# Hash attention and a gated feed-forward block: keys and queries of pairs one to four turned by VectorE from block loads, and another pace of weight pieces

## Chip, cores and metric

The kernel runs on one core of one Trainium2 chip. The metric is the device time of one execution in microseconds, as a median of several runs. Engines are named as the profile names them: PE is TensorE's matmul, PEld its weight load, DVE VectorE, ACT ScalarE, POOL GpSimd, SP SyncE; SPq and the like are the queues in which an engine issues its DMAs.

## What is computed

The inputs q, k and v have 4 batches, 8 heads, 768 positions and 64 columns. Each query and key gets a bucket from the signs of six projections, and attends only within its bucket. The result is rearranged to 3072 tokens of 512 columns and goes through a gated block with 1536 hidden columns.

```python
q_bits = (np.einsum('bhsd,dk->bhsk', q, proj) > 0)      # k_bits likewise
mask = q_bucket[:, :, :, None] == k_bucket[:, :, None, :]
scores = np.where(mask, scale * np.matmul(q, k.transpose(0, 1, 3, 2)), -1e9)
attn = softmax(scores)                                   # over the keys
x = np.matmul(attn, v).transpose(0, 2, 1, 3).reshape(B * S, H * D)
g = x @ w_gate
out = (g * (1.0 / (1.0 + np.exp(-g))) * (x @ w_val)) @ w_out
```

The three weights come as doubles. The kernel reads them as two 32-bit words per number and makes float parts of them itself.

## The kernel before

**Attention.** Two heads at a time make a pair; there are 16 pairs, numbered 0 to 15, four to a batch (`pairs`, L309). Each pair runs through these steps.

- `fetch` (L312) loads raw q, k and v. q and k have one buffer each (`bufs=1`, L323), v has two. For pairs 0 to 4 (`n <= NP`, L326) q and k come as rows, two DMAs a tensor, with runs of 64 floats. For pairs 5 to 15 (L332 to L340) they come in blocks of 32 by 32, four DMAs a tensor with runs of 32 floats, laid so that turning each block gives the operand with head and column on the partitions.
- `front(n)` (L420) returns the steps that make the operands. For pairs 0 to 4 `transpose` (L421) makes three 128x128 transposes on PE (L426) for each half of q and k, twelve a pair, and ACT copies each half out of PSUM (L429). For pairs 5 to 15 `transpose_blocks` (L478) turns q and k with one DVE instruction each (L480).
- `hash_next` (L468) projects q and k (four matmuls, L439) and ACT takes the signs (L444). The bits of q are copied to the second head's rows by a DMA in SP's queue (`spread_q`, L456). Those of k are written twice by ACT with a mask for pairs 1 to 4 (L475), and once by ACT and then spread by DVE (`spread_k`, L450 to L453) for pairs 5 to 15. Pair 0 has its own step, `hash_own` (L458).
- `score` (L502) multiplies q and k, adds the product of the bits in the same PSUM bank, and ACT takes the exponential (L515) into a ring of twelve units. There are twelve units a pair: two halves of the queries by six blocks of keys.
- `add` (L540) sums the exponentials on DVE (L547, L551, L554) and `total` (L559) sums them over the partitions on PE (L565). The sums go through SP's queue (`few`, L570), a reciprocal on DVE (L574), memory (`sums`, L576), and back, spread over the partitions (L583).
- `attend` (L518) multiplies the weights by v (av, L526). `norm` (L587, L590) scales the result, and for the first 1024 tokens `split` (L263) cuts it into three parts, with L283 on ACT and L287 and L292 on DVE.

**The order** is written out by hand and each engine works its queue in that order. The loop over pairs (L612) emits for pair n: the turn of pair n + 1 if that is DVE's, twelve scores with the adds between them, the turn if it is PE's, the total of pair n - 1, the hashing of pair n + 1, norm and reciprocal of earlier pairs, weight pieces, and av of pair n. The loads of pair n + 2 are emitted after the third score where DVE turns pair n + 1 (L628), and after PE's transposes otherwise (L632).

**Weight pieces.** There are 36 pieces. `load_words` (L119) reads one (L126), `scale` (L128) scales it on ACT (L135, L136), `widths` (L145) joins the words on DVE (L149, L151, L154), `round_up` (L139) rounds on ACT (L142), and `parts` (L159) makes the remaining parts on DVE (L162, L164) and writes the piece to memory (L166). So a piece has a first half of three DVE instructions, and in the next pair a second half of two. `PACE` (L609) says how many pieces are begun in each pair; 23 pieces are made in the attention. The other 13 are made in the gated block by `turns` (L212), a few steps after each atom of work. During attention POOL's queue issues the reads and writes of the pieces, and, in the last three pairs, reads of ring pieces (`bring`, L234, L244).

**Gated block** (L664). Three blocks of 1024 tokens. For each of the twelve groups of hidden columns the products `a` and `n` are made, and after every three groups the product `o`, all at L681.

Of the kernel before, what the change touches and what calls it, by code (L numbers as in the profile page):

```python
# [8 lines left out]
FP32 = mybir.dt.float32  # L9
# [10 lines left out]
def kernel(  # L20
# [20 lines left out]
    nc = tc.nc  # L41
    PSUM = bass.MemoryType.PSUM
    B, H, S, D = q.shape
    NBITS = proj.shape[1]
    P = 128
# [3 lines left out]
    BLOCK = 32  # L49
    NP = H // 2  # L50
# [12 lines left out]
    OFF = 2.0**35  # L63
# [234 lines left out]
    def attention(scope):  # L298
# [13 lines left out]
        def fetch(n, name, queue, half=None):  # L312
            b, pr = pairs[n]
            if name == "v":
                t = raws["v", n] = raw.tile([P, 2, NCH, D], FP32, tag="vraw", name="vraw")
                queue.dma_start(
                    t.rearrange("p h c d -> p h (c d)"),
                    v[b, 2 * pr : 2 * pr + 2].rearrange("h (p c) d -> p h (c d)", c=NCH),
                )
                return  # L320
            src = q if name == "q" else k
            if not half:
                raws[name, n] = raw.tile([P, NCH, 2, D], FP32, tag=name + "raw", name=name + "raw",  # L323
                                         bufs=1)
            t = raws[name, n]
            if n <= NP:  # L326
                cs = slice(None) if half is None else slice(half * CH, (half + 1) * CH)
                for h in range(2):
                    queue.dma_start(t[:, cs, h, :],
                                    src[b, 2 * pr + h].rearrange("(p c) d -> p c d", c=NCH)[:, cs, :])  # L330
                return
            blocks = t.rearrange("p c a b -> p (c a b)").rearrange(  # L332
                "p (c a d) -> p c a d", a=P // BLOCK, d=BLOCK)
            for h in range(2):
                for x in range(D // BLOCK):
                    at = h * D + x * BLOCK
                    queue.dma_start(  # L337
                        blocks[at : at + BLOCK],
                        src[b, 2 * pr + h][:, x * BLOCK : (x + 1) * BLOCK].rearrange(
                            "(a p c) d -> p c a d", c=NCH, p=BLOCK))  # L340

        def load(n, names):
            if n < len(pairs):
                for name in names:
                    fetch(n, name, nc.sync)
# [22 lines left out]

        HR = 16
        assert 2 * NBITS <= HR and 2 * HR == BLOCK  # L370
        rules = fixed.tile([BLOCK, 8, BLOCK], FP32, tag="rules", name="rules")
        NUDGE = -(2.0**-120)
        nc.gpsimd.memset(rules[:, 2:8, :], 0.0)
        nc.gpsimd.memset(rules[:, 0:2, :], NUDGE)
        groups = rules.rearrange("p x (g r) -> p x g r", r=HR)
        nc.gpsimd.memset(groups[:, 0, :, NBITS : 2 * NBITS], 1.0)
        nc.gpsimd.memset(groups[:, 1, :, NBITS : 2 * NBITS], -1.0)
        for h in range(2):
            nc.gpsimd.memset(groups[:, 2 + h, h, 0:NBITS], NUDGE)
            nc.gpsimd.memset(groups[:, 2 + h, h, NBITS : 2 * NBITS], -1.0)  # L380
            nc.gpsimd.memset(groups[:, 4 + h, h, 0 : 2 * NBITS], 1.0)
            nc.gpsimd.memset(groups[:, 6 + h, h, 0 : 2 * NBITS], OFF / 2)
        nc.vector.tensor_tensor(rules, rules,
                                ident[0:BLOCK, 0:BLOCK].unsqueeze(1).to_broadcast([BLOCK, 8, BLOCK]),
                                op=ALU.mult)
        columns = fixed.tile([P, 8], FP32, tag="columns", name="columns")
        nc.vector.tensor_reduce(out=columns[0:BLOCK], in_=rules, axis=AX.X, op=ALU.add)
        columns = [columns[0:BLOCK, x : x + 1] for x in range(8)]
        nudge = {"q": columns[0], "k": columns[1]}
        one_head = columns[2:4]  # L390
        mask, times_k = columns[4:6], columns[6:8]

        hash_w = fixed.tile([P, BLOCK], FP32, tag="hash", name="hash")
        nc.vector.memset(hash_w, 0.0)
# [15 lines left out]
            nc.gpsimd.memset(t, 0.0)  # L410

        load_words(2, nc.sync)
        for name, queue in (("q", nc.sync), ("k", nc.gpsimd), ("v", nc.sync)):
            fetch(1, name, queue)
        load_words(3)

# [3 lines left out]
        def front(n):  # L420
# [29 lines left out]
            def spread_k(times, cols=slice(0, S)):  # L450
                b = bits["k", n][:, cols]
                for to, by in ((high, times[1]), (low, times[0])):
                    nc.vector.tensor_scalar(b[to], b[low], scalar1=by, scalar2=None, op0=ALU.mult)  # L453
# [4 lines left out]
            def hash_own(*todo):  # L458
                for f in hash_blocks(todo):
                    f()  # L460
                for name, half in todo:
                    cols = slice(half * HQ, (half + 1) * HQ)
                    if name == "k":
                        spread_k(mask, cols)
                    else:
                        nc.vector.tensor_copy(bits["q", n][high, cols], bits["q", n][low, cols])

            def hash_next(todo):  # L468
                q0, q1, *ks = hash_blocks(todo)
                q0()  # L470
                q1()
                spread_q()
                if n > NP:
                    return ks + [lambda: spread_k(times_k)]
                return [lambda k=k, h=h: k(to=(low, high)[h], bias=one_head[h], scale=mask[h])  # L475
                        for k in ks for h in range(2)]

            def transpose_blocks(name):  # L478
                T[name, n] = opnd.tile([P, S], FP32, tag=name + "T", name=name + "T")
                nc.vector.transpose(T[name, n], raws[name, n].rearrange("p c h d -> p (c h d)"))  # L480

            order = [("q", 0), ("q", 1), ("k", 0), ("k", 1)]
            if n > NP:
                return [lambda name=name: transpose_blocks(name) for name in "kq"] + [
                    lambda: hash_next(order)]
            turns = [lambda x=x: transpose(*x) for x in order]
            if n == 0:
                return [turns[2], turns[0], lambda: hash_own(("k", 0)), lambda: hash_own(("q", 0)),
                        turns[3], turns[1], lambda: hash_own(("k", 1), ("q", 1))]
            return turns[2:] + turns[:2] + [lambda: hash_next(order)]  # L490

        units = [(n, half, c) for n in range(len(pairs)) for half in range(2) for c in range(NCH)]
        acc = {}
# [8 lines left out]
        def score(u):  # L502
            n, half, c = units[u]
            qs = slice(half * HQ, (half + 1) * HQ)
            ks = slice(c * P, (c + 1) * P)
            sc = [bank("sc")[:, 0:HQ] for _ in range(2)]
            for x, start in ((T, True), (bits, False)):
                if u < 2 and not start:
                    prepare_pair(1)
                for h in range(2):  # L510
                    rows = slice(h * D, (h + 1) * D)
                    nc.tensor.matmul(sc[h], x["k", n][rows, ks], x["q", n][rows, qs],  # L512
                                     start=start, stop=not start)
            for h in range(2):
                nc.scalar.activation(weights(u)[:, h, 0:HQ], sc[h], AF.Exp,  # L515
                                     scale=SCALE * (OFF / 2 if n <= NP else 1.0))

        def attend(u):  # L518
            n, half, c = units[u]
# [81 lines left out]
        def prepare_pair(count):  # L601
            for _ in range(count):
                if steps:
                    rest.extend(f for f in steps.pop(0)() or [] if f)
# [1 line left out]
        prepare_pair(4)  # L606
        finish(rest)
        last = []
        PACE = [2] * 4 + [1] * 3 + [2, 1] * 4 + [0]  # L609
        splits = []  # L610
        later = []
        for n in range(len(pairs)):  # L612
            u = 2 * NCH * n
            more = n + 1 < len(pairs)
            late = n + 1 > NP
            if n and more:
                steps = front(n + 1)
                if late:
                    prepare_pair(2)
            for i in range(2 * NCH):  # L620
                score(u + i)
                if u + i == 2:
                    prepare_pair(1)
                    finish(rest)
                    steps = front(n + 1)
                if i % NCH:
                    add(u + i)
                if late and i == 2:  # L628
                    load(n + 2, "qk")
            if more and not late:  # L630
                prepare_pair(4)
                load(n + 2, "qk")  # L632
            if n:
                total(n - 1)
            if more:
                prepare_pair(1)
            finish(rest)
            finish(last)
            while waiting:
                last.append(waiting.pop(0)())  # L640
            begin_pieces(PACE[n])
            finish(splits)
            splits.extend(later)
            later.clear()
            for c in range(2 * NCH):
                attend(u + c)
            load(n + 2, "v")
            advance_pieces()
            if n >= len(pairs) - 3:
                bring()  # L650
# [6 lines left out]

    with ExitStack() as scope:
        attention(scope)
        assert progress["kept"] == progress["scaled"]  # L660

# [231 lines left out]
```

## Time and profile before

| what | us |
|---|---|
| median of three runs | 933.76 |
| the three runs | 932.96, 933.76, 936.29 |
| the profiled execution | 932.62 |
| its span | 930.8 |
| attention: av of pair 0 begins | 24.00 |
| first product of the gated block | 329.66 |
| PE transposes L426, 60 of them, mean of one | 0.27 to 0.28 |
| DVE turns L480, k and q, eleven each, mean of one | 0.971 and 0.935 |
| k bits by ACT L444, mean of one | 0.612 |
| spread of k bits L453, 22 of them, mean of one | 0.408 |

The span runs from the first to the last instruction of the profiled execution; the execution is 1.82 us longer. Durations in the tables of the profile are those of single instructions, in microseconds from the start of the span, or in nanoseconds where that is said. Where several instructions of the same kind follow each other, a row gives the start of the first, the length of all, and their number after an x. Short instructions overlap at their edges, so a sum of means can exceed the length of the stretch. In the chain of work each piece is what released the next one; time that an engine spends outside the chain costs nothing.

### The profile page before, as it was taken

The page shows a single profiled execution, that of the slowest core. Times are in us where ns is not written, and L with a number is a line of the kernel's source. Part 1 is how long each engine was busy: PE and PEld are TensorE (multiplying, and loading weights), DVE is VectorE, ACT ScalarE, POOL GpSimd, SP SyncE. Part 2 cuts the span into 40 slices and gives each one's busy share as a digit, 9 for nine tenths or more (in the row PEclk, how much of TensorE's full clock was granted, in tenths as well). Part 3 has the DMA queues.
Part 4 walks back from the last instruction along what each step waited for, and adds up shares of the span by engine and source line. Part 5 has one row for each costly group of instructions (what it writes and reads, how often), then busy time and mean ns, then how long its engine had stood idle before and what let it go on. Part 6 is the DMA issues. An engine that isn't in the chain of part 4 may idle for free.

```text
span 930.8 us, 13055 instructions
## 1 busy us (share of the span) xinstructions
PE 919.3 (99%) x4837; PEld 643.0 (69%) x4837; DVE 655.4 (70%) x752; ACT 467.9 (50%) x838; POOL 92.9 (10%) x187
## 2 busy tenths in 40 slices
PE   8999999999999999999999999999999999999997
PEld 4444455444444478888888788888887888888886
DVE  5566899998998848779795855365568754474746
ACT  7899878887888645442523233331313233413220
POOL 3011001000101110010001000101000100001000
PEclk9999999999999999999999999999999999999999
DMA  6466767888788497685856563444434642525232
GB/s 170 113 207 179 189 162 191 217 198 197 220 239 210 172 315 288 221 327 201 307 203 230 198 257 106 170 136 150 154 137 148 235 142 100 199 69 205 101 136 90
DMA packets 131311, 174.28 MB, mean 187 GB/s; under 512 B 92400, under 2 KB 100816, under 8 KB 131248
## 3 DMA queue, kind: packets, MB, share of 16 engines
q0 software_dynamic: 22512, 116.01, 35.6%
q1 hardware_dynamic: 107936, 57.25, 22.9%
q8 instruction: 38, 0.62, 0.3%
q14 instruction: 25, 0.20, 0.1%
q10 hardware_dynamic: 800, 0.20, 0.1%
HBM read 133.17 MB, written 39.42 MB: 185 GB/s over the span
## 4 chain that ended last, share of the span: by engine, by line
PE 86%; DVE 6%; ACT 3%; DMA 2%; issue 2%; SPq 1%; DVEq 0%; ACTq 0%; POOLq 0%
PE a L681 25%; PE o L681 18%; PE sc L512 15%; PE n L681 13%; PE av L526 12%; ACT A L515 1%; PE hps L439 1%; PE sum L565 1%; SPq L337 1%; DVE v L730 1%; DVE v L726 1%; DVE hid L734 1%; DMA r<-sums 1%; DVE hid L736 1%; PE tps L426 1%
## 5 line engine op out<-in xcount | busy, mean ns | idle before, releaser
L681 PE MATMUL a<-xparts,ring 128*128 128x512 f32 x1152 | 277.0, 392 | 0.6 <-ACT row L568 0.6
L681 PEld LDWEIGHTS a<-xparts,ring 128*128 128x128 f32 x1152 | 216.2, 188 | 50.2 <-ACT row L568 1.3
L681 PE MATMUL o<-ring,hid 128*128 128x512 f32 x864 | 199.1, 390 | 1.3 <-DVE hid L736 1.1
L681 PEld LDWEIGHTS o<-ring,hid 128*128 128x128 f32 x864 | 161.8, 188 | 36.6 <-DVE hid L736 2.4
L515 ACT ACTIVATE A<-sc 128x384 f32<-128x384 f32 x384 | 157.3, 492 | 9.9 <-PE sc L512 9.7
L512 PE MATMUL sc<-qT,kT 64*128 64x384 f32 x768 | 157.2, 487 | 0.0
L681 PE MATMUL n<-xparts,ring 128*128 128x512 f32 x576 | 144.3, 393 | 0.0
L526 PE MATMUL av<-A,vraw 128*64 128x386 f32 (+1 forms) x768 | 127.7, 488 | 0.0
L681 PEld LDWEIGHTS n<-xparts,ring 128*128 128x128 f32 x576 | 108.1, 188 | 24.3
L726 DVE TENSOR_TENSOR v<-v,n 128x1024 f32<-128x1024 f32 x36 | 43.9, 1220 | 99.7 <-PE n L681 99.7
L244 POOL DMA_DIRECT2D ring<-ram x108 | 56.9, 529 | 510.4 <-PE n L681 331.9
L526 PEld LDWEIGHTS av<-A,vraw 128*64 128x64 f32 x768 | 53.7, 136 | 73.3 <-issue 64.0
L512 PEld LDWEIGHTS sc<-qT,kT 64*128 64x128 f32 x768 | 68.3, 187 | 49.4 <-issue 48.5
L720 ACT ACTIVATE g<-a 128x1024 f32<-128x1024 f32 x36 | 36.9, 1025 | 127.8 <-PE a L681 121.6
L731 ACT ACTIVATE hid<-v 128x1024 fp32r<-128x1024 f32 x36 | 38.2, 1061 | 115.1 <-DVE v L730 115.1
L728 ACT ACTIVATE g<-g 128x1024 f32<-128x1024 f32 x36 | 38.2, 1062 | 81.8 <-DVE g L726 81.8
L783 DVE TENSOR_TENSOR o<-o 128x512 f32<-128x512 f32 x92 | 63.0, 686 | 21.8 <-ACT o L777 19.5
L726 DVE TENSOR_TENSOR g<-g,n 128x1024 f32<-128x1024 f32 x36 | 43.7, 1215 | 34.6 <-PE n L681 34.6
L512 PE MATMUL sc<-qb,kb 64*128 64x384 bf16 x384 | 64.8, 323 | 2.4 <-DMA qb<-qb 1.5
L547 DVE SCALAR_TENSOR_TENSOR both<-A 128x1536 f32<-128x1536 f32 x32 | 55.8, 1745 | 13.4 <-ACT A L515 12.3
L734 DVE SCALAR_TENSOR_TENSOR hid<-hid,v 128x1024 fp32r<-128x1024 f32 x36 | 44.0, 1223 | 22.8 <-ACT hid L731 22.8
L551 DVE TENSOR_TENSOR both<-both,A 128x1536 f32<-128x1536 f32 x32 | 56.3, 1758 | 3.3
(79 smaller groups left out, 713.9 us busy)
## 6 DMA issues: line engine op xcount, KB each, us to landing
ring<-ram POOLq DMA_DIRECT2D x108, 768.0 KB, 4.7
ram<-stage POOLq DMA_DIRECT2D x23, 768.0 KB, 5.1
ram<-stage SPq DMA_DIRECT2D x13, 768.0 KB
vraw<-in_v_dram SPq DMA_DIRECT2D x16, 384.0 KB
out_dram<-o SPq DMA_DIRECT2D x24, 256.0 KB
r<-sums SPq DMA_DIRECT2D x30, 192.0 KB
qraw<-in_q_dram SPq DMA_DIRECT2D x48, 96.0 KB
words<-in_moe_w_gate_dram POOLq DMA_DIRECT2D x9, 512.0 KB, 7.6
```

The lines of the kernel that those rows point to most:

```text
L244: nc.gpsimd.dma_start(t.bitcast(FP32), ram[at].bitcast(FP32))
L512: nc.tensor.matmul(sc[h], x["k", n][rows, ks], x["q", n][rows, qs], start=start, stop=not start)
L515: nc.scalar.activation(weights(u)[:, h, 0:HQ], sc[h], AF.Exp, scale=SCALE * (OFF / 2 if n <= NP else 1.0))
L526: nc.tensor.matmul(ps[h * D : (h + 1) * D, 0:width], raws["v", n][:, h, c, :], a[:, h, 0:width], start=c == 0, stop=c == NCH - 1)
L547: nc.vector.scalar_tensor_tensor(out=t, in0=first, scalar=S * EPS / P / 2, in1=now, op0=ALU.add, op1=ALU.add)
L551: nc.vector.tensor_tensor(t, t, now, op=ALU.add)
L681: nc.tensor.matmul(ps, w, x, start=start, stop=stop)
L726: nc.vector.tensor_tensor(two(z), two(z), n_, op=ALU.subtract)
L728: nc.scalar.activation(z, z, AF.Silu)
L731: nc.scalar.activation(h, val, AF.Copy, scale=TOWARD / STEP)
L734: nc.vector.scalar_tensor_tensor(out=l, in0=h.bitcast(FP32), scalar=-STEP, in1=val, op0=ALU.mult, op1=ALU.add)
L783: nc.vector.tensor_tensor(accs[c], accs[c], t[:, 1], op=ALU.subtract)
```

## The change

Four things change.

- q and k of pairs 1 to 4 are loaded in blocks, four DMAs a tensor, and turned by DVE; all pairs but pair 0 now go this way. The bits of k are then written once by ACT and spread by DVE. Pair 1's k is loaded from SP's queue; it was POOL's.
- The turn of pair 1 and the loads of pair 2 are emitted after the ninth score of pair 0 (`TURN = 8`); from pair 1 on, the turn of the next pair stands ahead of the scores, and the loads after the third score.
- The masks for two heads (`one_head`) go, so the small table `rules` has six columns, not eight, and four small fills of POOL go.
- `PACE` of pairs 7 to 14 was 2, 1, 2, 1, 2, 1, 2, 1 and is 1, 2, 1, 2, 1, 2, 1, 2; pair 15 begins one piece where it began none. 24 pieces are begun in the attention, and the last of them gets its second half in the gated block.

```diff
-            if n <= NP:
+            if n == 0:
...
-        for name, queue in (("q", nc.sync), ("k", nc.gpsimd), ("v", nc.sync)):
+        for name, queue in (("q", nc.sync), ("k", nc.sync), ("v", nc.sync)):
             fetch(1, name, queue)
         load_words(3)
...
-                if n > NP:
-                    return ks + [lambda: spread_k(times_k)]
-                return [lambda k=k, h=h: k(to=(low, high)[h], bias=one_head[h], scale=mask[h])
-                        for k in ks for h in range(2)]
+                return ks + [lambda: spread_k(times_k)]
...
-            if n > NP:
+            if n:
                 return [lambda name=name: transpose_blocks(name) for name in "kq"] + [
                     lambda: hash_next(order)]
...
-                                     scale=SCALE * (OFF / 2 if n <= NP else 1.0))
+                                     scale=SCALE * (OFF / 2 if n == 0 else 1.0))
...
-        PACE = [2] * 4 + [1] * 3 + [2, 1] * 4 + [0]
+        PACE = [2] * 4 + [1] * 4 + [2, 1] * 4
+        TURN = 8
         for n in range(len(pairs)):
             u = 2 * NCH * n
             more = n + 1 < len(pairs)
-            late = n + 1 > NP
             if n and more:
                 steps = front(n + 1)
-                if late:
-                    prepare_pair(2)
+                prepare_pair(2)
             for i in range(2 * NCH):
                 score(u + i)
                 if u + i == 2:
                     prepare_pair(1)
                     finish(rest)
                     steps = front(n + 1)
+                if n == 0 and i == TURN:
+                    prepare_pair(2)
                 if i % NCH:
                     add(u + i)
-                if late and i == 2:
+                if i == (2 if n else TURN):
                     load(n + 2, "qk")
-            if more and not late:
-                prepare_pair(4)
-                load(n + 2, "qk")
```

More of the change, by code (lines that the diff above doesn't have):

```diff
@@ L370, in attention @@
         assert 2 * NBITS <= HR and 2 * HR == BLOCK
-        rules = fixed.tile([BLOCK, 8, BLOCK], FP32, tag="rules", name="rules")
+        rules = fixed.tile([BLOCK, 6, BLOCK], FP32, tag="rules", name="rules")
         NUDGE = -(2.0**-120)
-        nc.gpsimd.memset(rules[:, 2:8, :], 0.0)
+        nc.gpsimd.memset(rules[:, 2:6, :], 0.0)
         nc.gpsimd.memset(rules[:, 0:2, :], NUDGE)
@@ L378, in attention @@
         for h in range(2):
[L379 to L382, printed above, removed]
+            nc.gpsimd.memset(groups[:, 2 + h, h, 0 : 2 * NBITS], 1.0)
+            nc.gpsimd.memset(groups[:, 4 + h, h, 0 : 2 * NBITS], OFF / 2)
         nc.vector.tensor_tensor(rules, rules,
-                                ident[0:BLOCK, 0:BLOCK].unsqueeze(1).to_broadcast([BLOCK, 8, BLOCK]),
+                                ident[0:BLOCK, 0:BLOCK].unsqueeze(1).to_broadcast([BLOCK, 6, BLOCK]),
                                 op=ALU.mult)
-        columns = fixed.tile([P, 8], FP32, tag="columns", name="columns")
+        columns = fixed.tile([P, 6], FP32, tag="columns", name="columns")
         nc.vector.tensor_reduce(out=columns[0:BLOCK], in_=rules, axis=AX.X, op=ALU.add)
-        columns = [columns[0:BLOCK, x : x + 1] for x in range(8)]
+        columns = [columns[0:BLOCK, x : x + 1] for x in range(6)]
         nudge = {"q": columns[0], "k": columns[1]}
-        one_head = columns[2:4]
-        mask, times_k = columns[4:6], columns[6:8]
+        mask, times_k = columns[2:4], columns[4:6]
         hash_w = fixed.tile([P, BLOCK], FP32, tag="hash", name="hash")
@@ L486, in front @@
             turns = [lambda x=x: transpose(*x) for x in order]
[L487 to L490, printed above, removed]
+            return [turns[2], turns[0], lambda: hash_own(("k", 0)), lambda: hash_own(("q", 0)),
+                    turns[3], turns[1], lambda: hash_own(("k", 1), ("q", 1))]
         units = [(n, half, c) for n in range(len(pairs)) for half in range(2) for c in range(NCH)]
@@ L659 @@
         attention(scope)
-        assert progress["kept"] == progress["scaled"]
     def gated_block(scope):
```

## The prediction

> **What bounds the kernel now.** I read the page first, then busy time by stretch, then the chain that ended last, then the queues of VectorE (DVE) and SyncE (SP) around the pairs that change.
>
> The page's first lines say what kind of kernel this is:
>
> ```profile
> span 930.8 us, 13055 instructions
> PE 919.3 (99%) x4837; PEld 643.0 (69%) x4837; DVE 655.4 (70%) x752; ACT 467.9 (50%) x838; POOL 92.9 (10%) x187
> ```
>
> TensorE is busy nearly always, so work taken from it is worth its time unless a wait takes its place. Next, busy time cut where the av products of a pair begin (pair 1 at 45.20, pair 2 at 66.39, and so on; columns: stretch, length, then each engine):
>
> ```profile
> 45.20:66.39 21.19, 21.19 (x150) 10.52 (x152) 15.22 (x18) 19.95 (x44) 2.64 (x4) 1.00 0.64 202
> 66.39:87.58 21.19, 21.19 (x150) 10.51 (x152) 16.22 (x19) 19.95 (x44) 2.41 (x4) 1.00 0.65 201
> 87.58:106.81 19.23, 19.23 (x139) 9.21 (x140) 12.89 (x20) 18.99 (x42) 2.14 (x4) 1.00 0.70 188
> 106.81:128.00 21.19, 20.11 (x141) 10.38 (x142) 20.36 (x25) 17.08 (x39) 1.84 (x3) 1.00 0.75 201
> 147.91:167.13 19.22, 19.22 (x138) 9.19 (x140) 18.03 (x23) 16.07 (x37) 1.30 (x2) 1.00 0.77 179
> ```
>
> A cycle whose next pair is turned on TensorE takes 21.19 us, one whose next pair is turned by VectorE 19.23, and PE is full in both. The granted clock is 1.00 throughout. The exception is 106.81 to 147.91: two cycles in 41.10 us where 2 x 19.23 = 38.46 would do, 2.64 us too long. The chain says why:
>
> ```profile
> 63.00 1.46 PE tps L426 x12
> 64.46 0.78 PE sum L565 x8
> 65.24 1.15 PE hps L439 x8
> ...
> 105.39 0.78 PE sum L565 x8
> 106.17 0.65 PE hps L439 x8
> ...
> 114.98 1.95 DMA qb<-qb
> ```
>
> Ahead of pair 2's av stand 1.46 us of transposes and 1.15 of hashing, ahead of pair 4's only 0.65 of hashing. At 114.98, and again at 135.32, the scores wait for the copy of the q bits (L456), which stands in SP's queue behind the eight block loads of the pair after:
>
> ```profile
> 103.66 0.97 DVE L480 STREAM_TRANSPOSE kT<-kraw 128x768 f32<-128x768 f32 x1
> 104.55 0.94 DVE L480 STREAM_TRANSPOSE qT<-qraw 128x768 f32<-128x768 f32 x1
> ...
> 105.51 5.86 SPq L337 DMA_DIRECT2D qraw<-in_q_dram  x4
> 111.42 2.77 SPq L337 DMA_DIRECT2D kraw<-in_k_dram  x4
> ```
>
> (first two: timeline of DVE; last two: of SP's queue). Raw q and k have one buffer each, so the loads wait for the turn. From the end of the turn (105.49) to the bits landed (116.93) is 11.4 us; the next time 124.83 to 137.23, 12.4; later pairs lie between. Scores begin 19.23 us after those of the pair before and want the bits some 0.75 us later (two matmuls come first), so a turn that ends more than 19.98 - 11.4 = 8.6 (or 19.98 - 12.4 = 7.6) us after the scores begin makes PE wait. Call this lag S. It was 105.49 - 95.50 = 10.0 in pair 4; pair 7 has 162.2 - 155.82 = 6.4 and no wait.
>
> **The change part by part.**
>
> *TensorE's transposes of pairs 2, 3 and 4 go.* Each saves 12 transposes (1.46) and the wait for ScalarE's copies inside the hashing (1.15 - 0.65 = 0.50): 1.96 us, the difference of 21.19 and 19.23. Three of them lie on a full PE: 5.88 us. ScalarE also loses four copies (about 0.5 each, L429) and two net signs (0.61 each) per pair, off the path.
>
> *What VectorE gets.* Two turns, 0.97 + 0.94, and two spreads of the k bits (L453), 0.85 together: 2.76 us a pair. [...] But PE is the full engine and the chain passes through it, so I count PE's time if DVE keeps up. Does it? DVE's cycle from 105.41 to 124.76 is 19.35 us and holds adds (9.46), spread, norm, reciprocal, one split of x, the second halves of two weight pieces, the first half of one, and the turn. A first half more is 1.79 (100.08 to 103.66 for two), no split is 1.81 less, one second half less 1.33 less. So after the change: pair 2, two pieces and no split: 19.33; pair 3 with a split: 21.14; pair 4: 19.35; pairs 5 and 6: 18.0. Against 19.23 only pair 3 is clearly over, so DVE falls behind late and then recovers. With scores of pair 1 starting at 30.7 (below), I follow it: S is about 2 in pair 1, 3.8 in pair 2 (adds can't start before 4.4 us into the scores, since they wait for the exponentials), 4.4 in pair 3. In pair 4 the first split waits for ScalarE's L283: before, L287 began 95.54 - 87.58 = 7.96 after av; two signs fewer make it 6.4; the 9.9 us from there to the turn's end (95.54 to 105.45) give S = 6.4 + 9.9 - 7.91 = 8.4, on the edge: no wait at 11.4, 0.8 at 12.4. Pair 5: 8.4 + 19.35 - 19.23 = 8.5, and with 12.4 a wait of 1.0. Pair 6: under 7, none. So about 1.0 us of waiting remains of the 2.64: 1.6 gained. Bounds: nothing, and all of 2.64.
>
> *Pair 1's turn, inside pair 0.* Nothing in the trace shows block loads this early. SP can issue them from 10.66 (when q of pair 0 has been read); k now follows on SP, not on POOL. The eight took 6.35 us when nothing else moved (85.68 to 92.07) and 8.7 to 9.6 beside weight traffic; with some 2 us to land (the bits' copy takes 1.95) k is there at 19.0 to 22.3. VectorE is free at 19.76, so the turn ends at 21.7 to 24.2. The hashing follows (0.75), and av of pair 0 starts at 22.4 to 25.0; it starts at 24.00 now. DMA engines were busy until about 18 us, and the third weight load moves ahead of pair 1's loads: I take a turn ending at 22.0 and av at 22.8, nearer the quick end: 1.2 gained, bounds 1.6 gained and 1.0 lost. The second half of pair 0's adds queues behind the turn on DVE, by 1.9 us; DVE then idled 4.17 us before 28.77, which covers it.
>
> [...]
>
> *Bits of pair 1.* They now stand behind pair 2's eight loads, as new queue order: 22.0 + 6.4 + 2 = 30.4, wanted at 22.8 + 7.91 + 0.75 = 31.5. No wait if the loads are quick (DMA is idle from 19 to 24 now), 2.1 if they take 9.6. I count 0.3.
>
> *Pace.* One more first half of a piece (1.79) and a second half more (1.33) come in the last pair, and the weight load behind it stands in POOL's queue ahead of four ring loads. DVE idles 10.79 us there (325.9 to 336.73, waiting for the sums), which covers 3.1; the ring loads move by about 2 us, wanted from 340.67 and landing 4.7 after issue at 330. In the gated part two such halves change places and one piece fewer is begun, on a PE that is full: nothing. What may be late is the first o product (0.20 of waiting at 383.88): bounds 2.0 lost, 0.2 gained. I count 0.3 lost. Pairs 7 to 14 only swap which has two pieces: 17.5 us of DVE as a mean, under 19.23: nothing. The smaller rules table is hidden by the load of proj (to 4.75).
>
> Sum: 5.88 + 1.6 + 1.2 - 0.3 - 0.3 = 8.1 us. The profiled execution took 932.62 (span 930.8), giving 924.5; it lies 1.14 below the median of 933.76, so for the median I say 925.7.
>
> **Rivals.** *Waits eat the gain*: loads take 9.6 from the start, so pair 0 loses 1.0 and pair 1 waits 2.1, and nothing of the 2.64 goes: 5.88 - 3.1 = 2.8, 931.0. For it: 9.6 is seen beside weight traffic. Against: the weights rest at 19 to 28. *The last pair pays*: all else as forecast, but the shifted ring loads cost 2.0: 927.4. Against: the ring's slack of some 10 us. *Slower*: eight loads of 128-byte runs, beside two reads and two writes of weights a pair, take a time L far above 8.7 in pairs 1 to 4. Pair 1's bits then wait L - 7.5 (22.0 + L + 2 against 31.5), those of pairs 2, 3 and 4 each L - 13.8 (turn's end to landing is L + 2.8; S is 3.4 as a mean; 19.98 is allowed). Against the 7.1 gained on PE this decides from L = 14, and makes the kernel over 0.5% slower from 15.2. At 17.4, twice what was seen, it is 9.9 + 10.8 - 7.1 = 13.6 slower: 947.4. Against: pair 4 before had just this traffic and took 8.7. *No effect*, PE idling where the transposes were: the stretches with PE full, and 19.23 in ten later pairs under the same scheme, speak against it.
>
> **How the numbers follow.** Forecast 0.75 (923 to 928), last pair pays 0.08, waits eat the gain 0.12 (929.1 to 933), slower 0.05. Range 923.0 to 931.0: from the sum with every part at its good end (5.88 + 2.64 + 1.6 + 0.2 = 10.3, 923.5) to the case of the waits. A difference under 0.5% (4.7 us) can't be told from no change here: faster 0.83, same 0.12, slower 0.05.
>
> **What would show it.** Right: all cycles of pairs 0 to 3 at 19.23, no L426 beyond pair 0, av of pair 0 before 24.0, S under 5 in pairs 1 to 3 and a wait for qb only in pairs 5 and 6, about 1 us. Wrong: PE waiting for DVE L480 near 21 us or for qb near 31, block loads over 10 us, PE idle between 330 and 385.

## The result, and the profile after

The changed kernel takes 926.59 us as a median of six runs (924.02 to 927.82), the kernel before 933.08 beside it. The ratio is 0.9924, with a 95% interval of 0.9904 to 0.9943: faster, by 6.5 us where 8.1 was forecast (926.59 where 925.7 was). The profiled execution of the changed kernel took 927.82 (span 926.0), the longest of the six, so its waits are those of a bad case; a second profile (first experiment) shows another. First lines of the page after:

```profile
span 926.0 us, 12980 instructions
PE 912.7 (99%) x4789; PEld 638.9 (69%) x4789; DVE 666.4 (72%) x768; ACT 456.2 (49%) x814; POOL 91.6 (10%) x182
```

PE is busy for 6.6 us less, though a stretch at half clock, shown below, counts in it as busy. Busy time of the changed kernel, cut again where the av products of a pair begin (columns: stretch, length, PE, PEld, DVE, ACT, POOL, granted clock, DMA share, GB/s):

```profile
23.21:42.44 19.23, 19.23 (x138) 9.21 (x140) 15.78 (x18) 15.82 (x36) 1.51 (x2) 1.00 0.78 154
42.44:61.67 19.23, 19.23 (x138) 9.20 (x140) 17.64 (x22) 16.91 (x38) 2.64 (x4) 1.00 0.73 203
...
100.12:119.57 19.45, 19.45 (x139) 10.15 (x140) 18.72 (x24) 16.66 (x38) 1.84 (x3) 1.00 0.76 187
119.57:143.68 24.11, 21.23 (x139) 11.24 (x140) 21.24 (x25) 16.30 (x37) 1.30 (x2) 0.93 0.81 165
143.68:162.91 19.23, 19.23 (x138) 9.20 (x140) 17.51 (x22) 16.07 (x37) 1.30 (x2) 1.00 0.72 174
```

The cycles of 21.19 are 19.23 now. One stretch, from av of pair 5 to av of pair 6, takes 24.11, with PE idle for 2.88 of it and a mean clock of 0.93. The chain through it, and through pair 0:

```profile
15.80 4.38 DMA kraw<-in_k_dram
...
22.36 0.85 PE hps L436 x8
23.21 7.91 PE av L518 x48
...
127.77 3.55 DMA qb<-qb
131.32 0.04 issue
131.36 10.89 PE sc L504 x67
```

The k of pair 1 lands 4.38 us after its last load is issued. In pair 6 the copy of the bits (L453 here) takes 3.55 us, and the scores behind it 10.89 where the same 67 instructions took 9.20 before:

```profile
135.32 1.91 DMA qb<-qb
137.23 0.04 issue
137.28 9.20 PE sc L512 x67
```

Cutting that place of the changed kernel finely shows why:

```profile
127.50:131.36 3.86, 0.98 (x6) 0.31 (x6) 2.92 (x7) 0.97 (x2) 0.00 (x0) 1.00 0.36 57
131.36:134.80 3.44, 3.44 (x14) 2.25 (x15) 3.34 (x7) 1.36 (x3) 0.53 (x1) 0.51 0.54 121
134.80:142.20 7.40, 7.40 (x59) 4.83 (x56) 6.54 (x6) 7.18 (x18) 0.77 (x1) 1.00 1.01 266
```

After PE sat idle, the granted clock is 0.51 for 3.44 us and then 1.00 again. Half of 3.44 is an estimated 1.7 us lost on top of the wait.

The account of the two profiled executions, by the starts of av of a pair and of the gated block:

| stretch | before | after | gained |
|---|---|---|---|
| start to av of pair 0 | 24.00 | 23.21 | 0.79 |
| av of pair 0 to av of pair 3 | 63.58 | 57.68 | 5.90 |
| av of pair 3 to av of pair 4 | 19.23 | 19.23 | 0 |
| av of pair 4 to av of pair 6 | 41.10 | 43.56 | -2.46 |
| av of pair 6 to the gated block | 181.75 | 181.75 | 0 |
| gated block | 601.14 | 600.57 | 0.57 |

They add up to 4.80, which is 932.62 - 927.82.

### The profile page after: what moved, and what is told of

The parts are those of the page before. It is cut to its first block, busy times and chain, and to the rows that moved or that the text cites. A ratio compares the mean times of both kernels' runs of the same rounds, so it can differ in the third digit from the quotient of the medians.

```text
span 926.0 us, 12980 instructions
## 1 busy us (share of the span) xinstructions
PE 912.7 (99%) x4789; PEld 638.9 (69%) x4789; DVE 666.4 (72%) x768; ACT 456.2 (49%) x814; POOL 91.6 (10%) x182
## 4 chain that ended last, share of the span: by engine, by line
PE 95%; DVE 2%; DMA 1%; SPq 1%; issue 0%; ACT 0%; DVEq 0%; ACTq 0%; POOLq 0%
PE a L670 29%; PE o L670 19%; PE sc L504 16%; PE n L670 14%; PE av L518 14%; PE sum L557 1%; PE hps L436 1%; SPq L337 1%; DMA kraw<-in_k_dram 0%; DVE hid L725 0%; DVE v L715 0%; DVE hid L723 0%; DVE v L719 0%; DMA qb<-qb 0%; DMA proj<-in_proj_dram 0%
## 5 line engine op out<-in xcount | busy, mean ns | idle before, releaser
L723 DVE SCALAR_TENSOR_TENSOR hid<-hid,v 128x1024 fp32r<-128x1024 f32 x36 | 44.0, 1223 | 19.2 <-ACT hid L720 19.1
```

The costliest lines, as they stand in the source:

```text
L723: nc.vector.scalar_tensor_tensor(out=l, in0=h.bitcast(FP32), scalar=-STEP, in1=val, op0=ALU.mult, op1=ALU.add)
```

## Experiments

Theory A, as it stood after the first profile: the gain is PE's time, 5.9 us on a full PE, and 0.8 in pair 0; what is missing went into one wait of PE, in front of pair 6 for the bits of q, and into the half clock behind it. A1 says that the wait itself lowers the clock, A2 that the slow stretch has another cause. After r1 the wait of pair 0, for the turn of pair 1, joined the theory. Every run below stands beside runs of the kernel before on the same chip, which took 933.0 to 933.7 as a median; r1 to r4, r5 to r8 and r9 to r12 ran on three chips. Ratios are to that kernel, with their 95% interval.

**The changed kernel again** (r1).

> The changed kernel as it is, on the same chip as the three beside it. Theory A (the gain of about 6.5 us is 5.9 from the transposes of three cycles, 0.8 in pair 0 and 0.6 in the gated block, reduced because one wait for the bits of q in front of pair 6 grew from 1.3 to 3.1 us and the scores behind it ran at half clock for some 3.4 us): again 926 to 928, one stretch of about 24 us between the av of pairs 5 and 6, granted clock 0.5 behind the wait. Theory B (the long stretch was an accident of one profiled execution): the profile shows 19.2 to 20.5 there, and the time is the same as before.

925.30 us (923.44 to 927.65), 0.9917 (0.9902 to 0.9931). Theory A as it stood fell, and B came true: from av of pair 5 to av of pair 6 it is 19.9 us here, and the time is the same. The loss lies elsewhere in this execution (timeline of PE; in brackets the idle time before the row and what ended it):

```profile
23.30 0.52 PE L436 MATMUL hps<-qT,hash 128*32 128x384 f32 x2 [2.27 <-DVE qT L474]
...
131.26 0.32 PE L504 MATMUL sc<-qb,kb 64*128 64x384 bf16 x1 [0.36 <-DMA qb<-qb]
```

PE waited 2.27 for the turn and 0.36 for the bits, and it is av of pair 0 that ran slowly: 9.60 us, not 7.91, with 3.4 us of it at half clock. So there are two such places. The loss in pair 0 does not explain the short wait in pair 6: DVE's turn of pair 6 came later too, by 2.2 us, and ends 8.4 us after the scores begin, against 8.8. What was shorter is SP's queue and the copy:

```profile
119.12 5.91 SPq L337 DMA_DIRECT2D qraw<-in_q_dram  x4
125.07 3.13 SPq L337 DMA_DIRECT2D kraw<-in_k_dram  x4
...
128.99 2.22 DMA qb<-qb
```

The loads took 9.1 us, against 10.1, and the copy 2.22, against 3.55. In r8 below, av of pair 0 runs at full clock, and the wait in pair 6 is 0.19. Five profiles have this queue order and this pace up to pair 6 (the first, r1, r4, r8 and r10), and only the first shows the long wait. Why loads and copy were slow in that one stays open.

**Bits of q from ScalarE's queue** (r2).

```diff
-                nc.sync.dma_start(bits["q", n][high], bits["q", n][low])
+                nc.scalar.dma_start(bits["q", n][high], bits["q", n][low])
```

> One edit on the changed kernel: the copy of the q bits is issued from ScalarE's queue, right behind the signs that make them, and no longer from SyncE's behind the eight block loads. Theory A (the wait in front of pair 6 comes from the order of SyncE's queue): no wait for qb in any pair, every cycle 19.2, the wait of 3.1 and the half-clock loss of 1.7 gone: 4.8 us faster than the changed kernel, about 922. Rival (the copy is late because the DMA engines are full, whichever queue issues it): under 1.5 us gained, about 925.5 or more, and a wait for qb still there.

922.39 us (922.13 to 923.07), 0.9887 (0.9874 to 0.9899), 2.9 below r1. The only wait of PE after the ramp of pair 0 that the trace lists before the end of attention is this one, and the clock stays at 1.00:

```profile
22.00 0.52 PE L436 MATMUL hps<-qT,hash 128*32 128x384 f32 x2 [1.43 <-DVE qT L474]
```

Every cycle up to av of pair 14 takes 19.2. The queue's order is shown as the cause of the wait: DVE's turn of pair 6 comes as late as in the changed kernel (it ends at 117.2, against 116.86), SP's loads with it, and only the bits no longer stand behind them. Rows of SP's queue, and the copy in ScalarE's:

```profile
117.23 6.56 SPq L337 DMA_DIRECT2D qraw<-in_q_dram  x4
123.84 2.92 SPq L337 DMA_DIRECT2D kraw<-in_k_dram  x4
...
120.25 0.51 ACTq L453 DMA_DIRECT2D qb<-qb  x1
```

Not all of the 2.9 is the queue's. From av of pair 1 to the gated block r2's profile takes 277.92 us, the first one 282.99 and r1's 278.81. So against the bad execution the edit is worth 5.1, near the 4.8 expected, but against the ordinary one 0.9. The rest between r1's profile and r2's, 3.0 us, lies in pair 0, ahead of the first scores that need a copy which the edit moves: the wait there was 1.43 and not 2.27, PE reached it earlier, and the clock did not fall behind it. Whether that is chance is not shown.

**A lighter pair 3** (r3). PACE is 2, 2, 2, 1, 1, 1, 1, 2, 1, 2, 1, 2, 2, 1, 2, 1. So pairs 7 to 11 change as well, and pair 12 has two pieces in both; all of that lies behind the wait of pair 6.

```diff
-        PACE = [2] * 4 + [1] * 4 + [2, 1] * 4
+        PACE = [2] * 3 + [1] * 4 + [2, 1] * 2 + [2, 2, 1, 2, 1]
```

> One edit on the changed kernel: pair 3 begins one weight piece and not two, and pair 12 begins two; 24 pieces as before. Theory A (VectorE falls behind in pairs 3 and 4, so pair 6's turn ends 8.8 us into the scores of pair 5): the turn in pair 5 ends about 3 us earlier, 5.7 us into the scores, the bits are there in time, 4.8 us faster than the changed kernel, about 922. Rival (the wait is set by SyncE's loads beside the weights' traffic and not by when the turn ends): under 1.5 us gained.

923.03 us (922.08 to 925.16), 0.9895 (0.9881 to 0.9909), 2.3 below r1 where 4.8 was expected. The turn in pair 5 ends 4.9 us after the scores begin (115.3 - 110.4) and no wait for the bits is left. From av of pair 1 to the gated block it takes 277.90, as in r2. DVE's lag is thus the second half of the cause: either the queue or the lag can be taken away. The profiled execution, 925.08, waited 2.30 in pair 0; the hashing behind it took 1.30, not 0.85, and av of pair 0 9.10.

**A filled wait in pair 6** (r4).

```diff
+                if u == 6 * 2 * NCH and not start:
+                    ps = bank("idle")
+                    for _ in range(12):
+                        nc.tensor.matmul(ps, sides["k", 1][:, 0:P], sides["k", 1][:, 0:512],
+                                         start=True, stop=True)
```

> One edit on the changed kernel: twelve bf16 matmuls of 128x512 on old data, into a bank nobody reads, stand on TensorE between pair 6's first q-k products and their bits, where it waits for some 3 us. They do no part of the computation. Theory A1 (the idle stretch itself makes the granted clock fall): the wait stays about 3 us but the clock stays at 1.0 behind it, and the kernel is some 1.7 us faster than the changed one, about 925. Theory A2 (the slow scores behind the wait have another cause): granted clock 0.5 again, and no gain, or a loss of up to 2.6 us where the wait is shorter than the filler.

926.68 us (926.00 to 927.71), 0.9932 (0.9920 to 0.9944). Inconclusive on the clock. The copy of the bits was issued at 128.10 and would have landed near 130.0 (an estimate, with the 1.95 us of r8's copy), but the filler held PE until 131.9:

```profile
129.25 2.76 PE L505 MATMUL idle<-kb 128*128 128x512 bf16 x12
131.94 0.34 PE L509 MATMUL sc<-qb,kb 64*128 64x384 bf16 x2
```

The clock stayed at 1.00, but there was only a wait of about 0.9 us to fill, and the filler cost 1.9.

**The pace alone** (r5): the kernel before with the new PACE, and 24 pieces begun in the attention.

```diff
-        PACE = [2] * 4 + [1] * 3 + [2, 1] * 4 + [0]
+        PACE = [2] * 4 + [1] * 4 + [2, 1] * 4
...
-        assert progress["kept"] == progress["scaled"]
```

> The kernel before with nothing but the new PACE (pairs 7 to 14 swapped, one piece begun in pair 15). Prediction's theory (pairs 7 to 14 cost nothing, the last pair's 3.1 us of VectorE hide in 10.8 of idling, the ring loads have some 10 us of slack): within 1 us of the kernel before. Rival (the gated block's first 60 us profit from a piece that is half made, since the wait of 0.20 before the first o product and others vanish): 0.5 to 1 us faster. Rival (the last pair pays): 1 to 2 us slower.

931.87 us, 0.9987 (0.9977 to 0.9997): 1.2 us faster, between 0.3 and 2.1. In the profile the gated block takes 600.7 (929.8 - 329.12) against 601.14, and the wait of 0.20 before an o product is gone: 0.46 us. The profile's other 0.54 comes from shorter waits for the bits in pairs 5 and 6 (0.47 and 0.53, where the kernel before has 0.78 and 0.76), where the two paces are still the same, so it isn't shown to be the pace's. The extra half pieces of the last pair cost nothing: PE's only idle time there is the 0.64 before the first product of the gated block, as in the kernel before.

**The kernel before with the bits from ScalarE's queue** (r6).

The same edit as r2's.

> The kernel before with nothing but the copy of the q bits issued from ScalarE's queue. Theory A (the two waits of pairs 5 and 6, 2.64 us together, come from the order of SyncE's queue): 2.6 us faster than before, about 930.4, and 19.23 in both cycles. Rival (the turn is late for the hashing too, or the k bits are): under 1 us.

933.51 us, 1.0000 (0.9988 to 1.0012). The expectation fell. Two rows of PE's timeline say where the gain went:

```profile
116.26 0.34 PE L512 MATMUL sc<-qb,kb 64*128 64x384 bf16 x2 [0.63 <-DVE kb L453]
...
384.65 6.46 PE L681 MATMUL o<-ring,hid 128*128 128x512 f32 x27 [1.26 <-DVE o L783]
```

DVE is so late in pair 4 (10 us after the scores begin) that the spread of the k bits comes next: the gated block starts at 328.60, only 1.06 earlier than before. There the o products then wait 0.48 and 1.26, where the kernel before waited 0.20, and the block takes 603.0. Why it is worse there, when all that reaches it is 1 us earlier, stays open.

**An early turn** (r7), on r2.

```diff
-        for name, queue in (("q", nc.sync), ("k", nc.sync), ("v", nc.sync)):
+        for name, queue in (("q", nc.sync), ("k", nc.gpsimd), ("v", nc.sync)):
...
-        TURN = 8
+        TURN = 4
```

> Three edits on the changed kernel: q bits from ScalarE's queue, pair 1's k loaded from GpSimd's queue, and TURN = 4. Theory (in pair 0 TensorE waits 1.4 to 2.3 us for the turn of pair 1, because eight loads on one queue land k at 20.2 to 21.1; with k on a second queue it lands near 17 and the turn, after the first add, ends near 19): no wait of PE before pair 1's hashing, av of pair 0 near 21.4 to 21.9, 1 to 1.5 us faster than with the bits' queue alone, about 921. Rival (the DMA engines set when k lands, not the queue): same as with the bits' queue alone, 922.4.

921.36 us (921.14 to 922.77), 0.9879 (0.9866 to 0.9891), about 1 us better than r2, with intervals that overlap. The expectation missed the wait: in its profile, that of the longest execution, PE still waits 0.93 before the hashing. The profile names an exponential of ScalarE, which ends at 21.70; the turn of q ends at 21.57, and in r2 0.14 lies between the turn's end and the hashing, so the turn would have held it as long. k was turned at 18.49, but q had not landed: DVE waited 1.12 for it, until 20.59. Two waits of 0.24 and 0.26 for the spread k bits follow, in front of the scores of pairs 5 and 7.

**A filled wait in pair 0** (r8).

```diff
             def hash_next(todo):
+                if n == 1:
+                    ps = bank("idle")
+                    for _ in range(6):
+                        nc.tensor.matmul(ps, sides["k", 0][:, 0:P], sides["k", 0][:, 0:512],
+                                         start=True, stop=True)
```

> One edit on the changed kernel: six bf16 matmuls of 128x512 on old data, into a bank nobody reads, stand on TensorE ahead of pair 1's hashing, some 1.4 us in the 1.9 to 2.3 for which it waits there. They do no part of the computation. Theory A1 (an idle stretch of 2.3 us or more makes the granted clock fall to a half for about 3.4 us, one of 2.1 or less does not): the clock never falls in pair 0, av of pair 0 takes 7.9 us in the profile, and the slower executions of the changed kernel (up to 927.7) go: median 0.5 to 1.5 us below the changed kernel's 925.3, unless pair 5's wait grows by what pair 0 gives. Theory A2 (the clock falls there for another reason): as before, 923 to 928.

923.91 us (923.48 to 924.51), 0.9902 (0.9888 to 0.9917), with PE's timeline:

```profile
20.41 1.47 PE L469 MATMUL idle<-kb 128*128 128x512 bf16 x6
22.74 0.52 PE L436 MATMUL hps<-qT,hash 128*32 128x384 f32 x2 [0.85 <-DVE qT L479]
```

Work that the result doesn't need, laid into a wait that PE has anyway, makes the kernel no slower: its ratio is 0.0015 (1.4 us) under r1's, though the intervals overlap, and the spread shrinks from 4.2 us to 1.0. av of pair 0 takes 7.91. This agrees with A1; that r8's executions would have kept their clock without the filler is not ruled out by this run alone.

**The transposes back** (r9), on r2.

```diff
             def hash_next(todo):
+                if 2 <= n <= NP:
+                    for _ in range(4):
+                        ps = bank("tps")
+                        for i in range(CH):
+                            nc.tensor.transpose(ps[:, i * P : (i + 1) * P], ident, ident)
```

> On the kernel with the q bits issued from ScalarE's queue (922.4 us, no wait but pair 0's): twelve TensorE transposes of the identity, whose result nobody reads, ahead of the hashing of each of pairs 2, 3 and 4, where the old ones stood. The turn by VectorE stays; the dummies do no part of the computation, and ScalarE's copies don't come back. Theory A (what the change removes is PE time on a full PE): three times 1.46 us, 4.4 us slower, 926.8. Rival (part of that time was cover for a wait that comes anyway): under 3 us slower.

927.72 us (927.20 to 930.03), 0.9949 (0.9936 to 0.9962): 5.3 slower than r2. The chain, once for each of the three pairs:

```profile
42.04 1.46 PE tps L470 x12
43.50 0.78 PE hps L436 x8
44.28 7.91 PE av L523 x48
```

The cycle from 44.28 to the next av at 65.11 is 20.83, 1.60 more than 19.23: 1.46, and 0.13 more for the hashing. Three of them are 4.8; another 0.6 is pair 0, which began av at 23.46 and not 22.86. PE's time was on the path in full.

**The old pace in the changed kernel** (r10).

> The changed kernel with the old PACE, so the other half of the split of the change: block loads and turns without the new pace. The pace alone made the kernel before about 1.2 us faster (931.9 against 933.0 to 933.7). If the two parts add up: 1.2 us slower than the changed kernel, about 926.5. If the pace's gain was of the old arrangement alone: 925.3.

924.77 us (923.34 to 926.76), 0.9917 (0.9902 to 0.9932), the same as r1. The parts do not add up: alone the pace gave 1.2, here nothing that can be told. An o product waits 0.43 in its profile, so the pace is worth at most some tenths there, under the spread that pair 0 makes. In this execution a wait of 1.83 in pair 0 was followed by 9.61 us for av.

**A late turn** (r11), on r2: `TURN = 10`.

> On the kernel with the q bits issued from ScalarE's queue: TURN = 10, so the turn of pair 1 stands one add later on VectorE and TensorE waits about 3.0 us for it and not 1.4. Theory A1 (a wait this long makes the granted clock fall to a half for about 3.4 us): 1.6 us of wait and 1.7 of slow clock, 3.3 us slower than that kernel in every execution, about 925.7, and av of pair 0 takes some 9.6 us. Theory A2 (the clock has another cause): 1.6 us slower, about 924.0, av of pair 0 7.9 us.

925.95 us (925.55 to 927.05), 0.9931 (0.9917 to 0.9944): 3.6 slower than r2, as A1 has it and not A2.

```profile
23.46 0.52 PE L436 MATMUL hps<-qT,hash 128*32 128x384 f32 x2 [2.98 <-DVE qT L474]
...
24.25 9.67 PE L518 MATMUL av<-A,vraw 128*64 128x386 f32 x48
```

The granted clock behind the wait (columns as in the table of stretches above):

```profile
23.46:24.72 1.26, 1.25 (x12) 0.46 (x14) 1.26 (x1) 0.28 (x1) 0.00 (x0) 1.00 0.00 0
24.72:28.13 3.41, 3.41 (x14) 1.26 (x12) 1.81 (x4) 2.70 (x6) 0.00 (x0) 0.50 0.86 143
```

1.55 us more of waiting cost 3.6 in the medians (3.1 in the two profiles, up to the gated block), and 1.7 of that is av, of which 3.4 us run at half clock. The half clock began 1.26 us after PE had work again, when the wait was over.

**All that helped** (r12): r7 with r3's PACE.

> All that helped, together: q bits from ScalarE's queue, pair 1's k from GpSimd's queue, TURN = 4, and one piece begun in pair 3, two in pair 12. The first three gave 921.4 with waits of 0.24 and 0.26 for the spread k bits in pairs 4 and 6. If VectorE's lag sets these, they go: 0.5 us faster, 920.9. If not: 921.4.

920.92 us (920.72 to 921.29), 0.9873 (0.9859 to 0.9886): the lowest median of all, 12.2 below the kernel before (933.10 here). From av of pair 1 to the gated block it takes 277.90. One wait of PE is left in pair 0:

```profile
20.79 0.52 PE L436 MATMUL hps<-qT,hash 128*32 128x384 f32 x2 [0.28 <-DVE qT L474]
```

The last of the eight loads lands at 19.54 here and at 19.83 in r2, so the second queue hardly moved that. The gain is that k was there early, and its turn was done when q landed.

## Why the prediction was right, and where its sizes were off

The sum against two profiles of the changed kernel, in us gained over the kernel before:

| stretch | forecast | first profile | r1 |
|---|---|---|---|
| start to av of pair 1 (one cycle of 1.96, pair 0's 1.2) | 3.16 | 2.76 | 0.13 |
| av of pair 1 to the gated block (two cycles, 1.6, less 0.3 for pair 1's bits) | 5.22 | 1.47 | 5.65 |
| gated block (pace) | -0.3 | 0.57 | 0.52 |

Without any wait behind av of pair 1 (r2, r3, r12) the middle row would be 6.5. The mechanism was right: PE's time on a full PE, less the waits for DVE and SP. What the sum left out is the clock behind a wait. That r1 comes to 6.3 of the 8.1 is in part luck: the last two rows give 1.3 more than forecast, the first 3.0 less.

**Transposes of three cycles, 5.88.** Measured 5.90 in the account. r9 shows that 1.60 of each 1.96 is PE's own. The other 0.36 went with ScalarE's copies, which r9 does not bring back.

**DVE keeps up until pair 3.** The lag S was forecast as 2, 3.8, 4.4, 8.4 and 8.5 in pairs 1 to 5; the turns end 2.0, 3.8, 5.8, 8.7 and 8.8 us after the scores begin. Pair 3 came 1.4 us later than forecast, past the 5 that was named as a sign, and the others within 0.3; in pairs 1 to 4 PE waits for nothing (0.22 us are lost in pair 5's cycle).

**About 1.0 us of waiting remains.** Right in the ordinary case: against r2's 277.92 from av of pair 1 to the gated block, 0.9 is lost in r1, 1.0 in r8 and 0.8 in r10 (278.81, 278.95 and 278.74). In the first profile the term was mis-sized. The place was right (pair 6's bits), the lag was right, but the time from the turn's end to the bits landed was 14.5 us (116.86 to 131.32) and not 12.4. These rows of SP's queue in the changed kernel have it:

```profile
116.90 7.05 SPq L337 DMA_DIRECT2D qraw<-in_q_dram  x4
123.99 2.99 SPq L337 DMA_DIRECT2D kraw<-in_k_dram  x4
127.08 0.59 SPq L562 DMA_DIRECT2D few<-row  x1
127.77 0.59 SPq L453 DMA_DIRECT2D qb<-qb  x1
```

The eight loads took 10.1 us, a little over the 9.6 that had been taken as the worst, and the copy 3.55 and not 1.95. In r1 turn to landing took 12.1, in r8 11.9. So 2.46 was lost in that execution where 1.6 was to be gained, 1.7 of it by the clock, which the prediction left out altogether: the kernel before has no wait over 0.8 us from av of pair 0 to the gated block, and its clock is at 1.00 there.

**Pair 0, 1.2.** This is the term that was mis-sized in the ordinary case. Forecast: turn ends at 22.0, av at 22.8. Measured 22.2 and 23.2 in one profile, 23.2 and 24.2 in the other. The loads were issued as quickly as in the good case (6.0 us), but k landed 4.4 to 4.6 us after the last issue, where 2 had been taken from the copy of the bits; and the hashing took 0.85, not 0.75. The wait this leaves (1.9 to 2.3 us of PE) was in the forecast as a later av, but again not its clock. So the term was 0.8 gained in the first profile, and 1.8 lost in r1's, as 24.15 and 1.69 of slow av show. PE waiting for the turn near 21 us was one of the prediction's own signs of being wrong, and so were block loads of over 10 us; both came.

**Bits of pair 1.** No wait, as forecast: eight loads from 22.24 to 27.73, the copy at 27.85.

**Pace, -0.3.** The sign was wrong and the size small: +1.2 alone (r5), of which the gated block shows 0.5, and nothing to be told in company (r10). The cover named for it, DVE's idling ahead of the sums, held: 6.05 us of the 10.79 are left.

**Rivals.** No effect and slower are out. So is the last pair: no o product waits for it. Waits ate part of the gain, but not as that rival had it: the first loads took 6.0 us and not 9.6, and pair 1 did not wait.

The fall of the clock, all executions together (PE's wait, and the granted clock behind it):

| wait of PE, us | where | clock behind it |
|---|---|---|
| 0.28, 0.85, 0.93, 1.43 | r12, r8, r7, r2, pair 0 | 1.00 |
| 1.84, 1.86, 2.09 | r9, after, r4, pair 0 | 1.00 |
| 1.83 | r10, pair 0 | falls, av 9.61 |
| 2.27, 2.30 | r1, r3, pair 0 | falls, av 9.60 and 9.10 |
| 2.98 | r11, pair 0 | falls, av 9.60 |
| 2.88 | after, pair 6 | falls, 0.51 for 3.44 us |

Up to 1.43 us nothing happened, from 2.27 it happened each time, and between the two it went both ways, so the limit between 2.1 and 2.3 in r8's expectation does not hold. What made the difference between 1.83 us in r10 and 1.84 in r9 no run shows. The fall lasted 3.44 us in pair 6 of the first profile and 3.41 in r11, and in r1, r3 and r10 an estimated 3.3 to 3.4 (twice the time that the hashing and av of pair 0 lost). It began up to 0.3 us after the wait in r3 and in pair 6 of the first profile, 1.26 us after it in r11, an estimated 1.2 in r10 (mean clock 0.71 from 22 to 27 us), and in r1 behind the hashing, 0.85 or later.

The granted clock of the whole span, which is on record for every execution, agrees with A1 for the changed kernel and its variants: by an estimate one fall takes about 0.002 off it (half of 3.42 in 924). It is 0.998 or less in all five executions of r11 and in none of the 21 of r2, r7, r8, r9 and r12. Of the changed kernel's twelve it is so in six, which take 925.8 to 927.8 us; the other six take 923.4 to 926.3. At which wait it fell can be told for the profiled ones only. The kernel before, too, has 0.998 or less in five of the 43 executions beside r1 to r12; no profile shows those, so what lowered the clock in them stays open.

## What to carry to other kernels

Moving work off a full engine was worth its time on that engine here (5.90 us for three cycles; r9 put 1.60 of each 1.96 back), and it was the moved work's place in the other queues that decided what was kept: a small transfer that the full engine needs next should not stand behind large ones that nobody needs for a cycle (r2: 0.9 us from av of pair 1 to the gated block against the ordinary execution, 5.1 against the bad one). When a wait on TensorE nears 2 us, look at the clock behind it: here waits of 1.83 us and more could cost 1.7 us on top, and from 2.27 they did each time, 1.6 to 1.7 us. One that can't be removed can be filled with idle matmuls, if they are shorter than the wait: 1.47 us of them in r8 left a wait of 0.85 and av at 7.91, while the 2.76 us in r4 held PE an estimated 1.9 us too long. A wait seen in one profile is not a price until a second profile shows it: the one of 2.88 us in front of pair 6 did not come again, and the one that did lay in pair 0.

## What the runs showed of the hardware that was not expected

The granted clock fell to a half for about 3.4 us (3.41 in r11, 3.44 in the first profile) after PE waits as short as 1.83 us (r10). The price was 1.69 us for av of pair 0 (r1: 9.60 against 7.91), and it came on top of the wait. The fall began as late as 1.26 us after PE was at work again (r11). Of the eight block loads for pair 1, issued in 6.0 us, the last landed 4.38 us after its issue in the first profile; with k on another queue (r12), the last of q landed 6.85 after.
